# The first stage of a prime-factor Fourier filter on sixteen 32x32 tiles

## The chip, the cores and the metric

The kernel runs on one core of a Trainium2 chip. The metric is the device time of one launch in microseconds, the median of three runs. Everything is float32; a float32 matmul of the program appears in the trace as two matmul instructions.

## The reference

```python
batch, seq, dim = (8, 3008, 256)          # x; n_freq = 1505
X = np.fft.rfft(x, axis=1)
Y = X * (filt_r + 1j * filt_i)[None, :, :]
y = np.fft.irfft(Y, n=seq, axis=1)        # 24064 tokens of 256
h = y @ w_in                              # 256 -> 2048
g = h * np.clip(h + 3.0, 0.0, 6.0) / 6.0  # hardswish
out = g @ w_out                           # 2048 -> 256
```

Each of the 8 batches is filtered along its 3008 rows, every one of the 256 columns with a filter of its own. The filtered rows are the tokens of a two-layer network.

## The kernel before

**The network sets the order.** The 24064 tokens are 47 blocks of 512. A block is done in eight steps, one for each 256 of the 2048 hidden values, so there are 376 steps, numbered through; "step 42" is block 5, slice 2. In a step TensorE makes the seven products of a Strassen-like scheme for the first layer of its slice (`up_1` to `up_5`, tiles `al` and `be`) and the seven for the second layer of the slice before (`down`, tiles `po`). The last up-product of a step reads `xn` and writes `al`; it is the mark from which step lengths are counted here. ScalarE and VectorE make the hardswish. `t_sums` on GpSimd makes the operand sums of a block (`xt`), which the next block reads. Products go through `strips`, whose matmul is line 832.

**The filter is fitted between the steps.** 3008 is 47 x 64. For batch b:
- *First stage*, `a6_unit` (batches 2 to 7) and `a_unit` (batch 1): for each of the 64 residues c, a transform over the 47 rows 64a + c to frequencies k = 0 to 23, as matmuls with K = 47 against table `wa`, in which the twiddle factors are folded. A chunk of six columns is loaded by `x_load` and done by 12 matmuls of a 64x64 tile, 256 columns each; the last chunk of a batch has two columns and 4 matmuls. `a6_sums` makes sums and differences of the two halves on VectorE, `z6_store` writes them to DRAM (`z_d`) on GpSimd's queue. Batches 2 to 7 have six chunks each, at steps `A_AT` after the start of the seventh block ahead of the batch's first block.
- *Second stage*: `t2_load` reads z back, `b_unit` makes the 64-point transforms, `f_unit` and `y_unit` multiply with the filter on VectorE, `bi8_unit` makes the inverse 64-point transforms as 16 matmuls of a 32x32 tile with 512 columns, `bi8_sums` the sums of its halves, `g8_store` writes g to DRAM. The filter's rows come through `table_load` into two buffers `ft`: in batch 1 in 16 small transfers a table (lines 280 and 281) straight from the filter, and `table_store` then writes them to `f_d`; later batches read `f_d` in one transfer.
- *Last stage*: `t4_load` reads g (lines 731 and 742), `n_five` and `n_unit` make the last inverse transforms, whose output goes to `xn`, the tokens' ring.

Batch 0 goes through a path of its own before the steps; batch 1's first stage is in steps 2 to 9, its second in steps 12 to 34.

**Order by hand.** A dictionary `plan` says which functions a step calls and in which of five places. Place 3 stands at the beginning of a step, ahead of its up-products (`bi8_unit` stands there), place 4 just behind it, place 0 in the middle, place 1 later (`a6_unit`), place 2 at the end: loads, stores, sums. Within a place the order is that in which `at` was called. Each engine, and each queue of transfers, works through its instructions in this order. Transfers issued by `nc.sync` are on SP's queue: all loads, and the stores of the output in `store` (lines 1016, 1019 and 1024, once a block). Those by `nc.gpsimd` are on GpSimd's queue.

`late(i)` moves one VectorE operation (`g_last`) of a step that follows heavy VectorE work (`HEAVY`) behind `up_3`. After a unit in place 3, `inverse` picks the order of the down-products.

Of the kernel before, what the change touches and what calls it, by code (L numbers as in the profile page):

```python
# [42 lines left out]
SIX = tuple(range(0, HC, 6))  # L43
# [41 lines left out]
def _make_tables():  # L85
# [53 lines left out]
    def terms(k, j, at):  # L139
        m = (2.0 if k else 1.0) / N  # L140
        t0, t1 = ([2 * np.pi * ((at(j, h, a) * k) % N) / N for h in range(2)])
        c0, s0, c1, s1 = m * np.cos(t0), m * np.sin(t0), m * np.cos(t1), m * np.sin(t1)
        z = np.zeros(NA)
        if j:
            return {(0, 0): (c0, c1), (0, 1): (s0, -s1), (1, 0): (-c0, c1), (1, 1): (-s0, -s1)}
        return {(0, 0): (c0, z), (0, 1): (z, c1), (1, 0): (z, -s1), (1, 1): (-s0, z)}
# [11 lines left out]
    groups = np.zeros((P, HC, NA))  # L158
    ones = np.zeros((P, 2, TOK))
# [3 lines left out]
    for k in range(KH):  # L163
        for j in range(HC):
            for (ri, hh), x in terms(k, j, rows).items():
                if j in FIRST:
                    first[hh * 64 + ri * 32 + k, FIRST.index(j)] = first_of(x, FIRST.index(j))
                if j < 2:
                    ones[ri * ATOM + hh * KH + k, j] = cs_of(x)
            if j in FIRST:  # L170
                for (ri, hh), x in terms(k, j, late_rows).items():
                    last[ri * ATOM + hh * KH + k, FIRST.index(j)] = cs_of(x)
            if j > 1:
                cs = [terms(k, j, rows)[0, hh][0] for hh in range(2)]
                for ri in range(2):
                    c, s = cs[ri], cs[1 - ri]
                    pair_ = (c, s) if j < QC else ((c + s) / 2, (c - s) / 2) if j == QC else (c, -s)
                    for hh in range(2):
                        groups[ri * HALF + hh * KH + k, j] = pair_[hh ^ ri]
        if k >= KH - TC:  # L180
            for q in range(64):
                fr = k + NA * q if q < 32 else NA * (q - 31) - k
                for n, j in enumerate(FIRST):
                    th = [2 * np.pi * ((fr * rows(j, h, a)) % N) / N for h in range(2)]
                    direct[at_of[q], k - KH + TC, n * TOK:(n + 1) * TOK] = 2 / N * first_of(np.cos(th), n)
                    direct[HALF + at_of[q], k - KH + TC, n * TOK:(n + 1) * TOK] = -2 / N * first_of(np.sin(th), n)
    wai = np.concatenate([t.reshape(P, -1) for t in (groups, ones, first, last)], axis=1)
    f = np.float32
    return tuple(t.astype(f) for t in (wa, w0, wai, wi, wi2, wf, start, direct))


@with_exitstack
def kernel(
# [11 lines left out]
    wa_np, w0_np, wai_np, wi_np, wi2_np, wf_np, start_np, direct_np = _make_tables()  # L205
    wa_d = nc.inline_tensor(wa_np, name="wa_t").ap()
    w0_d = nc.inline_tensor(w0_np, name="w0_t").ap()
    wai_d = nc.inline_tensor(wai_np, name="wai_t").ap()
    wi_d = nc.inline_tensor(wi_np, name="wi_t").ap()
# [9 lines left out]
    f_d = nc.dram_tensor("f_tmp", (NT, P, TC * D), FP32, kind="Internal").ap()  # L219

# [39 lines left out]
    b12 = const.tile([P, P], FP32, name="b12")  # L260
    half_c = const.tile([P, 1], FP32, name="half_c")
# [34 lines left out]
    def table_store(c):  # L296
        nc.gpsimd.dma_start(f_d[c], ft[(NT + c) % FB].rearrange("p k d -> p (k d)"))
# [109 lines left out]
    def x_at(b, c):  # L407
        if b == 1:
            return xs[:, (b * NB + c) % 3, :, :], c * XC, XC
        t = xs.rearrange("p i j d -> p (i j) d")  # L410
        return t[:, ds((b * len(SIX) + c) % 2 * 6, 6), :], SIX[c], min(6, HC - SIX[c])

    def x_load(b, c):
        t, c0, n_ = x_at(b, c)
        rows = x[b].rearrange("(a c) d -> a c d", c=NC)
        for h in range(2):
            for r, n in ((0, 32), (32, NA - 32)):
                nc.sync.dma_start(t[h * 64 + r:h * 64 + r + n, 0:n_, :], rows[r:r + n, ds(h * HC + c0, n_), :])

# [58 lines left out]
    def a_unit(b, c):  # L482
# [8 lines left out]
        for h in range(2 if b == 1 and c < NB - 2 else 1):  # L491
            copy(c == NB - 2, t[:, :, h, :], ps[h])
# [3 lines left out]
    def a_sums(b, c):  # L496
        t, ps = st["t1", b, c]
        if b == 1:
            if c >= NB - 2:
                nc.vector.tensor_copy(out=t[:, :, 1, :], in_=ps)  # L500
            return
        nc.vector.tensor_tensor(out=t[:, :, 1, :], in0=t[:, :, 0, :], in1=ps, op=ALU.subtract)
        nc.vector.tensor_tensor(out=t[:, :, 0, :], in0=t[:, :, 0, :], in1=ps, op=ALU.add)

    def a6_unit(b, c):
        xc, c0, n = x_at(b, c)
        n //= 2
        t = t3p.tile([P, 4, 2, D], FP32, name="t3")[:, 0:3] if n == 3 else t1p.tile([P, 2, 2, D], FP32, name="t1")
        banks = [psF.tile([P, 512], FP32, name="psf", tag="f") for h in range(2)]
        be = psU.tile([P, 512], FP32, name="be") if n == 3 else None  # L510
        for r in range(n):
            for g in range(2):
                for h in range(2):
                    j, ps, o = (2, be, h) if r == 2 - 2 * h and n == 3 else (r - h if n == 3 else 0,) + (banks[h], r - h if n == 3 else 0)
                    q = g * n + j
                    nc.tensor.matmul(ps[ts(g, 64), ts(o, D)], wa[ds(h * 64, NA), ds((c0 + q) * 2 * KH, 64)],  # L516
                                     xc[ds(h * 64, NA), q, :], start=True, stop=True)
            if n == 3 and r == 0:
                nc.vector.tensor_copy(out=t[:, 2, 1, 0:2], in_=be[:, D:D + 2])
        m = min(n, 2)  # L520
        two = [ps[:, 0:m * D].rearrange("p (j d) -> p j d", d=D) for ps in banks]
        nc.scalar.activation(out=t[:, 0:m, 0, :], in_=two[0], func=AXT.Copy)
        if n == 3:
                nc.scalar.activation(out=t[:, 2, 1, 2:D], in_=be[:, D + 2:], func=AXT.Copy)
        st["t1", b, c] = t, be, two[1], n

    def a6_sums(b, c):
        t, be, ps, n = st["t1", b, c]
        v, m = nc.vector, min(n, 2)
        if n == 3:  # L530
            v.tensor_tensor(out=t[:, 2, 0, :], in0=be[:, 0:D], in1=t[:, 2, 1, :], op=ALU.add)
            v.tensor_tensor(out=t[:, 2, 1, :], in0=be[:, 0:D], in1=t[:, 2, 1, :], op=ALU.subtract)
        v.tensor_tensor(out=t[:, 0:m, 1, :], in0=t[:, 0:m, 0, :], in1=ps, op=ALU.subtract)
        v.tensor_tensor(out=t[:, 0:m, 0, :], in0=t[:, 0:m, 0, :], in1=ps, op=ALU.add)

    def z6_store(b, c):
        t, _, _, n = st.pop(("t1", b, c))
        for g in range(2):
            for ri in range(2):
                p0 = g * 64 + ri * KH  # L540
                nc.gpsimd.dma_start(z_d[b, :, ri, ds(SIX[c] + n * g, n), :, :].rearrange("k j s d -> k (j s d)"),
                                    t[p0:p0 + KH, 0:n, :, :].rearrange("p j s d -> p (j s d)"))
# [24 lines left out]
    def b_unit(b, i):  # L567
        c, r = divmod(2 * i, TC)
        if b != 1:
# [8 lines left out]
            else:  # L578
                for ri in range(2):
                    for s_ in range(2):  # L580
                        for v in range(2):
                            for k in range(2):
                                nc.tensor.matmul(ps[k][ds(v * 64 + s_ * 32, 32), ts(ri, D)], wf[ts(k, 64), s_, ts(ri, 32)],  # L583
# [66 lines left out]
    def bi8_unit(b, r):  # L650
        ys = [st.pop(("y", b, 2 * r + h)) for h in range(2)]
        even = [psU.tile([P, 512], FP32, name=x) for x in ("al", "be")]
        odd = [psF.tile([P, 512], FP32, name="psf", tag="f") for v in range(2)]
        for h in range(2):
            for ri in range(2):
                for v in range(2):
                    for par, ps in enumerate((even[v], odd[v])):
                        q = ds(v * HALF + par * HC, HC)
                        nc.tensor.matmul(ps[ds(h * HALF + ri * HC, HC)].rearrange("p (k d) -> p k d", k=2), wi2[q, ri, :],  # L659
# [384 lines left out]
    def at(step, fn, *a):  # L1044
        plan.setdefault((step, 0 if fn in EARLY else 1 if fn in (w_scale, a6_unit) else 2), []).append((fn, a))

    with tc.manual_schedule():
# [110 lines left out]

        def wai_load():
# [61 lines left out]
        A_AT = (4, 6, 10, 12, 14, 15)  # L1221
# [10 lines left out]
        at(n_at[TAIL - 2] + 1, lambda: nc.sync.dma_start(edge, wai_d[:, ds(NW + ND, ND)]))  # L1232
        at(LAST * NP + 3, b12_back)
        prev = None
        for n in range(1, B):
            a_at, f_at, y_at, bi_at = places(n)
            for c, s in enumerate(a_at):
                at(s, a_unit if n == 1 else a6_unit, n, c)
                at(s, a_sums if n == 1 else a6_sums, n, c)
                at(s, *((z_store, n, c, nc.sync) if n == 1 else (z6_store, n, c)))  # L1240
                if c >= (3 if n == 1 else 2):
                    at(max(a_at[c - 3 + (n > 1)], s - 6), x_load, n, c)
                elif n > 1:
                    at(max(prev[-1 if n == 2 else c - 2], s - 6), x_load, n, c)
            for c in range(NT):
                s = f_at[2 * (c - TB) + (n == 1)] + 1 if c >= TB else a_at[-1] + (1, 3, 5)[c] if n > 1 else a_at[-1] + 1
                at(s, t2_load, n, c)
                s = f_at[2 * (c - FB) + 1] + 1 if c >= FB else a_at[-1] + (1, 2, 4)[(c + 1) * (n > 1)]
                at(s, table_load, n, c)
                if n == 1:  # L1250
                    at(f_at[2 * c], table_store, c)
# [14 lines left out]
            prev = a_at  # L1266
# [3 lines left out]
        HEAVY = (f_unit, y_unit, a_sums, n_five, a6_sums, bi8_sums)  # L1270
# [5 lines left out]
        for i in range(len(items) + 1):  # L1276
# [23 lines left out]
            inverse = bi8_unit in units  # L1300
# [90 lines left out]
```

## Time and profile before

| | |
|---|---|
| runs | 2588.89, 2586.48, 2588.42; median 2588.42 us |
| profiled execution | 2587.13 us, span 2585.3 us, TensorE's clock 0.999 of full |
| TensorE busy | 2568.9 us, 99% |
| VectorE, ScalarE, GpSimd busy | 1926.3 (75%), 1291.5 (50%), 463.3 us (18%) |
| transfers | 202.48 MB, 121574 packets |
| first stage of batches 2 to 7 (L516) | 768 matmul instructions of 47x64 |
| inverse 64-point (L659) | 672 matmul instructions of 32x32, batches 1 to 7 |

Busy times are for the whole span; the DMA line of the page has the mean share of 16 engines in 40 slices of 65 us each. In groups of instructions the columns are line, engine, operation, output<-input, shape, count, then busy us, mean ns of one, and the engine's idle time before. In timelines they are start and length in us, engine, line, operation, output<-input, count; issues that follow one another are merged with their gaps.

### The profile page before, as it was taken

How to read it: one execution, taken by the hardware profiler on the slowest of the kernel's cores; microseconds unless marked ns; L12 is line 12 of the kernel's file. 1: busy time of each engine (PE TensorE's matmuls, PEld its weight loads, DVE VectorE, ACT ScalarE, POOL GpSimd, SP SyncE). 2: the span in 40 equal slices, each digit the busy share in tenths (PEclk: the TensorE clock that was granted, in tenths of full speed). 3: DMA queues.
4: the chain of work that ended last, by engine and by line, in shares of the span. 5: the costliest groups of instructions: out<-in, count | busy, mean ns of one | idle time of the engine just before them, and what ended most of it. 6: DMA issues, size and time to landing. Idle time of an engine off the chain costs nothing.

```text
span 2585.3 us, 87840 instructions
## 1 busy us (share of the span) xinstructions
PE 2568.9 (99%) x38466; PEld 2046.5 (79%) x38466; DVE 1926.3 (75%) x3554; ACT 1291.5 (50%) x2668; POOL 463.3 (18%) x699
## 2 busy tenths in 40 slices
PE   8999999999999999999999999999999999999999
PEld 4488778878788887888878878788777887888887
DVE  6978777777767777687776887767777677766666
ACT  4554455545545445554455545554445554555554
POOL 3252021110311203112031120311112111111110
PEclk9999999999999999999999999999999999999999
DMA  8733332222332223222232222322222222110000
GB/s 237 220 107 98 85 103 89 67 64 69 86 89 66 75 59 90 84 67 74 60 91 82 72 77 59 85 83 72 84 55 82 82 75 65 41 45 25 20 22 26
DMA packets 121574, 202.48 MB, mean 78 GB/s; under 512 B 18290, under 2 KB 86352, under 8 KB 120806
## 3 DMA queue, kind: packets, MB, share of 16 engines
q1 hardware_dynamic: 105453, 148.27, 20.0%
q0 software_dynamic: 15456, 48.35, 6.6%
q8 instruction: 302, 4.95, 0.8%
q14 instruction: 82, 0.67, 0.1%
q10 hardware_dynamic: 281, 0.24, 0.0%
HBM read 121.38 MB, written 87.13 MB: 81 GB/s over the span
## 4 chain that ended last, share of the span: by engine, by line
PE 99%; DVE 1%; issue 0%; ACT 0%; POOL 0%; POOLq 0%; DVEq 0%
PE po L832 45%; PE al L832 26%; PE be L832 19%; PE psf L583 1%; PE psn L772 1%; PE psf L516 1%; PE al L659 1%; PE al L772 1%; PE be L516 1%; PE psf L591 0%; PE psf L489 0%; PE psf L644 0%; PE psn L832 0%; PE po L576 0%; PE al L1093 0%
## 5 line engine op out<-in xcount | busy, mean ns | idle before, releaser
L832 PEld LDWEIGHTS po<-w_all,g 128*64 128x64 f32 x20808 | 1244.5, 137 | 247.2 <-issue 24.4
L832 PE MATMUL po<-w_all,g 128*64 128x128 f32 (+1 forms) x20808 | 1419.8, 274 | 1.5 <-issue 1.5
L885 DVE SCALAR_TENSOR_TENSOR g<-r,h 128x512 f32<-128x512 f32 x736 | 526.1, 715 | 221.1 <-ACT r L880 217.2
L880 ACT ACTIVATE r<-h,half_c 128x512 f32<-128x512 f32 x736 | 530.9, 721 | 306.4 <-DVE h L861 294.3
L832 PE MATMUL al<-xt,w_all 128*64 128x256 f32 x4416 | 668.7, 380 | 0.1
L832 PE MATMUL be<-xt,w_all 128*64 128x256 f32 x2944 | 444.8, 379 | 0.0
L861 DVE TENSOR_TENSOR h<-be,s 128x512 f32<-128x512 f32 x368 | 253.9, 690 | 164.8 <-PE be L832 146.8
L832 PEld LDWEIGHTS be<-xt,w_all 128*64 128x64 f32 x2944 | 213.8, 137 | 104.2
L875 ACT ACTIVATE h<-al 128x256 f32<-128x256 f32 x368 | 141.0, 383 | 288.1 <-PE al L832 285.2
L832 PEld LDWEIGHTS al<-xt,w_all 128*64 128x64 f32 x4416 | 280.2, 137 | 3.2 <-POOL w_all L393 1.0
L866 DVE TENSOR_TENSOR h<-al,s 128x256 f32<-128x256 f32 x368 | 156.3, 425 | 151.8 <-PE al L832 147.8
L893 DVE TENSOR_TENSOR g<-g 128x512 f32<-128x512 f32 x367 | 255.6, 697 | 12.6
L832 PE MATMUL al<-xn,w_all 128*64 128x256 f32 (+1 forms) x1536 | 240.7, 392 | 1.0 <-DVE g L885 0.6
L827 POOL TENSOR_TENSOR xt<-xn 128x256 f32<-128x256 f32 x184 | 140.9, 785 | 558.1 <-ACT xn L752 558.1
L832 PE MATMUL be<-xn,w_all 128*64 128x256 f32 (+1 forms) x1536 | 238.3, 389 | 0.0
L847 ACT ACTIVATE s<-be 128x256 f32<-128x256 f32 x368 | 141.1, 383 | 176.6 <-PE be L832 176.6
L856 ACT ACTIVATE s<-al 128x256 f32<-128x256 f32 x368 | 141.2, 384 | 174.6 <-PE al L832 174.5
L846 ACT ACTIVATE s<-al 128x256 f32<-128x256 f32 x368 | 141.8, 385 | 110.9 <-PE al L832 110.9
L892 DVE TENSOR_TENSOR g<-g 128x256 f32<-128x256 f32 x367 | 162.5, 443 | 12.6
L832 PEld LDWEIGHTS be<-xn,w_all 128*64 128x64 f32 x1536 | 110.1, 137 | 63.5 <-issue 7.4
L898 DVE TENSOR_TENSOR g<-g 128x256 f32<-128x256 f32 x367 | 156.1, 425 | 4.1
L676 POOL DMA_DIRECT2D g_tmp<-t x84 | 44.9, 544 | 586.0 <-DVE t L670 583.3
(171 smaller groups left out, 1720.5 us busy)
## 6 DMA issues: line engine op xcount, KB each, us to landing
g_tmp<-t POOLq DMA_DIRECT2D x96, 256.0 KB, 4.4
t<-z_tmp SPq DMA_DIRECT2D x42, 512.0 KB
t<-g_tmp SPq DMA_DIRECT2D x168, 120.0 KB
ft<-f_tmp SPq DMA_DIRECT2D x36, 512.0 KB
z_tmp<-t POOLq DMA_DIRECT2D x120, 144.0 KB, 3.7
o_tmp<-o SPq DMA_DIRECT2D x46, 256.0 KB
xs<-in_x_dram SPq DMA_DIRECT2D x60, 192.0 KB
out_dram<-o SPq DMA_DIRECT2D x165, 47.0 KB
```

Of the source, the lines that this page charges most:

```text
L832: nc.tensor.matmul(ps[ds(o, STRIP)], w[:, ds(o, STRIP)], x, skip_group_check=True, **kw)
L846: nc.scalar.activation(out=s[:, 0, :], in_=al, func=AXT.Copy)
L847: nc.scalar.activation(out=s5, in_=be[:, 1, :], func=AXT.Copy)
L856: nc.scalar.activation(out=s[:, 1, :], in_=al, func=AXT.Copy)
L861: nc.vector.tensor_tensor(out=st["h"][0].rearrange("p (a n) -> p a n", a=2), in0=be, in1=s, op=ALU.add)
L866: nc.vector.tensor_tensor(out=st["h"][1][:, 256:512], in0=al, in1=s5, op=ALU.add)
L875: nc.scalar.activation(out=st["h"][1][:, 0:256], in_=al, func=AXT.Copy)
L880: nc.scalar.activation(out=r, in_=st["h"][i], func=AXT.Relu, bias=half_c, scale=1.0 / 6.0)
L885: nc.vector.scalar_tensor_tensor(out=st["g", k, p][:, o:o + 2, :].rearrange("p a n -> p (a n)"), in0=st["r", i], scalar=1.0, in1=st["h"][i ...
L892: v.tensor_tensor(out=g[:, G1, :], in0=g[:, G3, :], in1=g[:, G22, :], op=ALU.add)
L893: v.tensor_tensor(out=g[:, G3:G2 + 1:2, :], in0=g[:, G3:G1 + 1, :], in1=g[:, G11:G11 + 1, :].broadcast_to([P, 2, 256]), op=ALU.subtract)
L898: nc.vector.tensor_tensor(out=g[:, G4, :], in0=g[:, G12, :], in1=g[:, G2, :], op=ALU.subtract)
```

## The change

For batches 2 to 7 the two transforms of 47 and 64 points are arranged in prime-factor order: row index n goes to (t, u) with n = 64t + 47u modulo 3008, and no twiddle factors are left between the stages. Rows that mirror each other in t (t and -t) then meet the same cosine and the opposite sine. So the first stage needs 24 sums (against cosines) and 24 differences (against sines) in place of 47 rows.

- `half_load` brings in, for 8 values of u at a time on four groups of 24 partitions, the rows and the mirrored rows: 8 transfers a chunk, 4 chunks a batch. `half_sums` makes sums and differences on GpSimd, four operations of 128x512.
- `a8_unit` does a chunk in 16 matmuls of a 32x32 tile (K = 24) over 512 columns, in place 3; `a8_sums` and `z8_store` take the places of `a6_sums` and `z6_store`. `A_AT` has four steps instead of six.
- Rows that wrap around the end of x are made contiguous by copies in DRAM: nine `x_twice` of 376 rows and eight `x_back` of 192 rows a batch, on SP's queue, some 50 to 30 steps ahead of their batch (for batch 2 from step 6).
- The frequencies are permuted, so the filter's tables are, too: 280 `filter_move`s copy runs of filter rows from the inputs to `f_d`, eight in each step from step 10 on, on SP's queue; in `plan` they stand behind `t4_load` and ahead of the other loads of their step. Batch 2 corrects signs (`table_sign`, VectorE) and stores the tables; batch 1 no longer stores them.
- Tables for the last stage are reloaded between batch 1 and batch 2 (`groups_load`); `wf2` and `wi2p` stand in for `wf` and `wi2`.

The diff, cut to its core:

```diff
+    def filter_move(n):
+        k, ri, par, (i, m, at_, step) = FILTERS[n]
+        c, r, v = k // TC, k // 2 % 2, k % 2
+        h = D // 2
+        o = c * P * TC * D + (v * HALF + par * 32 + i) * TC * D + (2 * ri + r) * D
+        nc.sync.dma_start(bass.AP(tensor=f_d.tensor, offset=f_d.offset + o, ap=[[h, 2], [TC * D, m], [1, h]]),
+                          raw((filt_r, filt_i)[ri], at_, [[h, 2], [step * D, m], [1, h]]))
+    def table_sign(b, c):
+        for r in range(2):
+            t = st["ft", b, c][:, 1, r, :]
+            nc.vector.tensor_scalar(out=t, in0=t, scalar1=sgn[:, ds(2 * c + r, 1)], scalar2=1.0, op0=ALU.mult, op1=ALU.mult)
+    def x_twice(b, i):
+        rows = lambda t, o: t[ds(o, XCUT)].rearrange("(r m) d -> r (m d)", m=4)
+        nc.sync.dma_start(rows(x_d[b - 2], i * XCUT), rows(x[b], (XLOW + i * XCUT) % N))
+    def x_back(b, i):
+        u = 8 * i
...
+        nc.sync.dma_start(xb_d[b - 2, :, ds(u, 8), :].rearrange("t u d -> u t d"), src)
+    def half_load(b, m, d):
...
+        for r in range(4):
+            u = 8 * m + 4 * (r % 2) + HC * (r // 2)
+            to = t[ds(32 * r, KH), :, :]
+            if d:
+                nc.sync.dma_start(to, xb_d[b - 2, :, ds(u, 4), :])
+                continue
...
+    def half_sums(b, m):
+        t0, t1 = halves(b, m)
+        s_ = slots[2]
+        for i in range(2):
+            u = ts(i, 2)
+            nc.gpsimd.tensor_tensor(out=s_[:, u, :], in0=t0[:, u, :], in1=t1[:, u, :], op=ALU.add)
+        for i in range(2):
+            u = ts(i, 2)
+            nc.gpsimd.tensor_tensor(out=t0[:, u, :], in0=t0[:, u, :], in1=t1[:, u, :], op=ALU.subtract)
-    def a6_unit(b, c):
...
-                    nc.tensor.matmul(ps[ts(g, 64), ts(o, D)], wa[ds(h * 64, NA), ds((c0 + q) * 2 * KH, 64)],
-                                     xc[ds(h * 64, NA), q, :], start=True, stop=True)
...
+    def a8_unit(b, m):
+        xs_ = slots[2], next(halves(b, m))
+        first_ = [psU.tile([P, 512], FP32, name=n) for n in ("al", "be")]
+        ps = first_ + [psF.tile([P, 512], FP32, name="psf", tag="f") for h in range(2)]
+        for ri in range(2):
+            for v in range(2):
+                for r in range(4):
+                    nc.tensor.matmul(ps[r][ds(ri * HALF + v * 32, 32)].rearrange("p (e d) -> p e d", e=2),
+                                     wcs[ds(32 * r, KH), ri, :], xs_[ri][ds(32 * r, KH), ts(v, 2), :], start=True, stop=True)
+        t = t3p.tile([P, 4, 2, D], FP32, name="t3").rearrange("p (r e) s d -> p r e s d", r=2)
+        for r in range(2):
+            nc.scalar.activation(out=t[:, r, :, 1, :], in_=ps[r].rearrange("p (e d) -> p e d", e=2), func=AXT.Copy)
...
-        A_AT = (4, 6, 10, 12, 14, 15)
+        A_AT = (4, 7, 13, 21)
...
+        for i in range(len(FILTERS)):
+            at(10 + i // 8, filter_move, i)
...
+                load = a_at[0] - 5 if c == 0 else a_at[c - 1] - 1
+                at(a_at[c] - 2, half_sums, n, c)
+                for d in range(2):
+                    at(load, half_load, n, c, d)
+                plan.setdefault((s, 3), []).append((a8_unit, (n, c)))
+                plan.setdefault((s, 4), []).append((a8_sums, (n, c, 0)))
+                at(s, a8_sums, n, c, 1)
+                at(s, z8_store, n, c)
+            for i in range(XCUTS if n > 1 else 0):
+                at(a_at[0] - (51 if n > 2 else 30) + 3 * i // 2, x_twice, n, i)
+            for i in range(8 if n > 1 else 0):
+                at(a_at[0] - (37 if n > 2 else 16) + i, x_back, n, i)
```

## The prediction

> **What bounds the kernel now.** I read the page first, then TensorE's timeline step by step, then the SP queue's timeline where the change adds transfers, then GpSimd's groups. The page (total, busy time, chain of waits):
>
> ```profile
> span 2585.3 us, 87840 instructions
> ...
> PE 2568.9 (99%) x38466; PEld 2046.5 (79%) x38466; DVE 1926.3 (75%) x3554; ACT 1291.5 (50%) x2668; POOL 463.3 (18%) x699
> ...
> PE 99%; DVE 1%; issue 0%; ACT 0%; POOL 0%; POOLq 0%; DVEq 0%
> ```
>
> TensorE is the chain from end to end and idles 16 us in all. So an edit is worth what it takes out of TensorE's stream, less what it makes TensorE wait. The stream is read off by steps: each step has one last up-product `al<-xn`, and the distance between two of them is the price of the step between.
>
> ```profile
> 353.93 0.60 PE L832 MATMUL al<-xn,w_all 128*64 128x256 f32 x4
> ...
> 360.00 0.60 PE L832 MATMUL al<-xn,w_all 128*64 128x256 f32 x4
> ...
> 367.72 0.65 PE L832 MATMUL al<-xn,w_all 128*64 128x256 f32 x4
> ...
> 500.04 0.60 PE L832 MATMUL al<-xn,w_all 128*64 128x256 f32 x4
> ...
> 501.45 0.61 PE L659 MATMUL al<-y,wi 32*32 32x512 f32 x1
> ...
> 507.48 0.65 PE L832 MATMUL al<-xn,w_all 128*64 128x256 f32 x4
> ```
>
> A bare step takes 6.08 (353.93 to 360.00). Step 42 carries an `a6_unit` of six columns: 360.00 to 367.72, 7.72. Step 63 carries a `bi8_unit`: 500.04 to 507.48, 7.44. In the same view step 47, with the two-column `a6_unit`, takes 6.82 (396.87 to 403.69), and the step after any of them 6.13. A unit on top of an `n_five` costs the same (9.18 against 7.54).
>
> **The change part by part.**
>
> *First stage on TensorE.* Removed per batch: five units at 7.72 - 6.08 = 1.64, one at 0.74, and 0.05 in each of six steps behind: 9.24 us. Added: four `a8_unit`. The trace does not have them, but it has their twin: `bi8_unit` is also 16 matmuls of a 32x32 tile over 512 columns in four banks, with two ScalarE copies and four VectorE sums of 128x512. So 7.44 - 6.08 = 1.36, plus 0.05 behind: 4 x 1.41 = 5.64. Gain 3.60 a batch, six batches: **21.6 us**. It lies wholly on the path.
>
> *VectorE and ScalarE.* Per batch VectorE had five times (2 x 0.43 + 2 x 0.68 + 0.16) and 0.84, 12.7 us; it gets 16 x 0.69 = 11.0. ScalarE's copies stay near 5 us. Both stay beside TensorE's work. `table_sign` adds twelve VectorE passes of 128x256 in batch 2; the nearest row is a 128x512 TENSOR_SCALAR of 0.47, so 0 to 5 us; VectorE is free a quarter of the time: I take 1.
>
> *GpSimd.* `half_sums` adds four 128x512 operations a unit. From these rows
>
> ```profile
> L827 POOL TENSOR_TENSOR xt<-xn 128x256 f32<-128x256 f32 x184 | 140.9, 785 | 558.1 <-ACT xn L752 558.1
> L393 POOL TENSOR_TENSOR w_all<-w_all 128x128 f32<-128x128 f32 x64 | 34.7, 562 | 18.2 <-DVE w_all L385 15.8
> ```
>
> (shape, count, busy us, mean ns, idle before) the line is 0.22 per 128 columns, so 1.23 for 512 and 4.9 us a unit. The tightest place is a batch's second unit, three steps behind the first. GpSimd first issues the first unit's z stores; behind a `bi8_unit` such four issues end 4.8 us into the next step (565.97, the step from 561.2). The sums end at 9.7; the unit starts 6.13 + 6.08 + 1.4 = 13.6 us into that stretch (1.4 is 500.04 to 501.45 above). Cover: 3.9 us, and `t_sums` behind it still ends a step before its use. I cost it at nothing; without that cover each microsecond would cost six.
>
> *The SP queue, once, in batch 1's stage.* Here the change adds most: 280 `filter_move`s, eight a step from step 10, plus `x_twice`, `x_back` and `half_load`. They stand in program order ahead of the filter and g loads of their step. This is the queue of before (start, length, line, count):
>
> ```profile
> 148.52 0.38 SPq L557 DMA_DIRECT2D t<-z_tmp  x1
> 148.96 0.67 SPq L280 DMA_DIRECT2D ft<-in_filt_r_dram  x1
> ...
> 174.12 6.09 SPq L742 DMA_DIRECT2D t<-g_tmp  x10
> ...
> 205.02 4.86 SPq L1019 DMA_DIRECT2D out_dram<-o  x7
> ```
> ```profile
> 256.30 6.60 SPq L1019 DMA_DIRECT2D out_dram<-o  x8
> 262.94 6.29 SPq L418 DMA_DIRECT2D xs<-in_x_dram  x8
> ```
>
> It issues without a break from 148.5 to 213.9, already, because batch 1's `table_load` is 16 issues of 0.64 each. What has to be out in time is `half_load` of batch 2's second chunk (step 35, behind 26 x 8 = 208 moves). Its unit stands at step 39. Without a stall step 36 begins at 318.7, then 7.44 + 6.13 + 7.54 give 339.8, the unit 1.4 later, the half that reads the differences 0.45 later: 341.7. Less 4.9 for the sums and 2.2 for landing (from a filter load's issue to its semaphore's last update in the trace): issued by 334.6. The queue is free from 146.5, so it has 188.1 us. Against that, from the timeline: tables, z and g loads 148.5 to 204.4, 55.9; store of block 1 6.3; four g loads 3.1; fifth table 11.5; sixth 10.9; stores of blocks 2 and 3 7.4 and 5.1; eight g loads 3.2; new half loads 16 x 0.41 = 6.6; fifteen new copies and a table x 0.44 = 6.6; and after each of three stores a pause of 3.0 (eight x loads took 6.29 where 8 x 0.41 = 3.3 would do). Sum 125.6. Left: 62.5 us, 0.30 a move. The queue's two waits of before (to 225.9 and 239.8, for a table's buffer) are gone by then, since it comes later than that.
>
> So TensorE waits 208 x f - 62.5, with f the time of a move in the queue. No row has such a move (two by up to 17 half rows, DRAM to DRAM). The rows near it (ns min/median/max):
>
> ```profile
> L731 SPq DMA_DIRECT2D t<-g_tmp x80: 289/314/1077, 210.8 to 2410.6; - x80
> ...
> L742 SPq DMA_DIRECT2D t<-g_tmp x200: 289/371/1793, 74.0 to 2305.7; - x100
> ```
> ```profile
> L280 SPq DMA_DIRECT2D ft<-in_filt_r_dram x24: 577/592/1602, 149.0 to 244.0; - x24
> ```
>
> With 0.045 between issues: 0.33 for the fastest, 0.36 for one-dimensional loads, 0.42 (0.44 in the mean from start to start, the odd long one included) for two-dimensional ones, 0.64 for pieces of the filter. A gain is excluded: an issue takes time and replaces none. I take **0.44**, the two-dimensional loads' mean, as the move has two dimensions: 91.5 - 62.5 = **29.0 us** of waiting, most at step 36, the rest at 39. Bounds: 0.33 gives 6, 0.64 gives 71. Behind the late half load the queue holds the g loads of step 38, which are due later; GpSimd, waiting for the half load, holds `t_sums` of block 5, whose 5.5 us still fit beside step 39's 7.4. At step 36 GpSimd's g stores (to 317.1) would make the unit 1.4 late by themselves; that lies inside the wait.
>
> [...]
>
> *Later batches.* The SP queue gets some 25 more issues a batch, 10 us in about 300, of which more than half are idle: nothing. That is 5 MB more data per batch, for engines whose digits on the page's DMA line are mostly 2 and 3 tenths: nothing. The x loads of batches 2 to 7 go, and `groups_load` reloads tables between batch 1's chunks, one issue each: nothing.
>
> *Sum.* -21.6 + 29.0 + 1 = +8.4 on the profiled run's 2587.1 (span 2585.3 and 1.8 around it). The median of the runs is 1.3 above that run: 2588.4 + 8.4 = **2597**.
>
> **The rivals.** *A, faster: the moves are cheap.* If a move costs 0.33 to 0.36, the wait is 6 to 12: 2588.4 - 21.6 + 10 + 1 = 2578. It decides from f = 0.37 down. For it: the 24-row loads at 0.36, and 60 us of idle queue between 214 and 320. Against: ten two-dimensional loads took 6.09, 0.61 each, in this very stretch. With moves at next to nothing it would be 2588.4 - 21.6 + 1 = 2568; no row is that low, and 0.02 of A's chance is for it. [...]
> *B, slower still: moves cost as filter loads,* 0.64: 2588.4 - 21.6 + 71 + 1 = 2639. For it: the same source rows; against: those loads write every second partition, moves none.
> *C: the sums on GpSimd run late in every batch.* If an add takes 3 us (VectorE's L885 rises from 0.69 to 0.93 us where GpSimd adds run beside it, so they do share something), 12 us exceed the 8.8 by 3: 6 x 3 on top, 2615. Against: GpSimd's adds have a longest of 1.23 at 256.
> *D: the new unit is no cheaper than the old,* 1.64: gain 14.9, 2604. Against: the twin's 21 units all cost 1.36 or a little more.
>
> **How the numbers follow.** Forecast (f 0.40 to 0.50, its own range 2589 to 2610) 0.45; A 0.30, B 0.14, C 0.07, D 0.04. The range reaches over A's and C's times and B's beginning: 2571 to 2625. 0.2% is 5.2 us, about what a measurement can tell from no change. Faster than that: A but for its upper edge, 0.28. Within: that edge and the third of the forecast near f = 0.40, 0.17. Slower: the rest, 0.55.
>
> **What would show it.** Steps with an `a8_unit` 7.44 long, their neighbours 6.1. The SP queue without a gap from 146 to some 390, moves about 0.44 apart. TensorE idle before the units of steps 36 and 39, released by GpSimd's sums, and those by a load; no such idle time from batch 3 on. Wrong would be: idle time before units of later batches (C), moves 0.35 or 0.6 apart (A, B), or a wait at another place, such as VectorE for `ft` in steps 12 to 30.

## The result and the profile after

The changed kernel takes **2691.8 us** (four runs, 2689.1 to 2697.2) where the one before takes 2587.5: a ratio of 1.041, 95% interval 1.039 to 1.043. I had forecast 2597, at most 2625. The page of the changed kernel (total, busy times, TensorE and its clock in 40 slices, chain of waits):

```profile
span 2691.7 us, 88272 instructions
...
PE 2586.7 (96%) x38466; PEld 2033.6 (76%) x38466; DVE 2001.1 (74%) x3500; ACT 1288.4 (48%) x2650; POOL 587.4 (22%) x747
...
PE   8998759999999999999999999999999999999998
...
PEclk9999879999999999999999999999999999999999
...
PE 85%; SPq 6%; DVE 6%; DMA 2%; issue 1%; ACT 0%; POOL 0%; POOLq 0%; DVEq 0%
```

TensorE was 99% of the chain; now SP's queue and VectorE have 6% each. The fourth to sixth slices of TensorE (8, 7, 5 tenths) are batch 1's stage, where I expected a wait, but a far longer one. VectorE's 6% are spread over all later batches, where I expected nothing.

The steps, as before by their last up-product, show that the unit itself is not the trouble. Step 87, which carries an `a8_unit`, and step 88 (TensorE's timeline):

```profile
744.53 0.60 PE L914 MATMUL al<-xn,w_all 128*64 128x256 f32 x4
...
752.12 0.65 PE L914 MATMUL al<-xn,w_all 128*64 128x256 f32 x4
...
758.25 0.60 PE L914 MATMUL al<-xn,w_all 128*64 128x256 f32 x4
```

It takes 7.59, the step behind it 6.13; I had 7.44 and 6.13. Comparing all 375 step lengths of the two traces splits the difference of the two spans, 106.4 us. (The split between units and sums takes the kernel both_out from below, which has the units but neither moves nor sums to speak of.)

| part | forecast | measured |
|---|---|---|
| units, steps 40 to the end | -21.6 | -19.1 |
| waiting up to step 39 (SP's queue) | +29 | +78.5 |
| `half_sums` on GpSimd, steps 40 to the end | 0 | +45.0 |
| behind the last matmul | 0 | +3.4 |
| signs (forecast); start-up (measured) | +1 | -1.4 |
| sum | +8.4 | +106.4 |

In both_out only 17.4 of the 19.1 lie in the steps that had or have a unit; the rest are a few other steps that happen to be shorter (step 306 by 1.1, step 100 by 0.7). The signs have no row of their own; what they cost lies in the other rows. Nor is all of the 78.5 idle time: up to step 39 TensorE is busy for 297.7 of 363.3 us, before for 283.5 of 284.9, so it idles 64 us more, and another 14 us are products at half clock: the granted clock is 0.50 for 6.8 to 20.5 us at each of the five longest waits, from a point within the wait on.

**Where SP's queue made TensorE wait.** Step 23 is 9.1 us longer than before, 29 13.9, 31 9.2, 36 23.7, 38 18.3. Waits in that stretch (engine and line, what released it, total, times, longest):

```profile
PE al L604 <- POOL xs L515: 20.4, 1, 20.4
...
PE psn L854 <- DMA t<-g_tmp: 17.0, 2, 15.9
...
DVE s L682 <- DMA ft<-in_filt_i_dram: 16.8, 2, 8.5
DVE s L682 <- DMA xb_tmp<-x_tmp: 14.0, 1, 14.0
```

Line 682 is `f_unit`: VectorE waits for batch 1's own filter tables in steps 23, 29 and 31, because the moves stand ahead of them. (In step 29 the trace names another transfer on the same semaphore.) The waits in steps 36 and 38 are those of the first unit and of an `n_five`. The cause is the price of a move, in the queue's row for `filter_move`:

```profile
L358 SPq DMA_DIRECT2D f_tmp<-in_filt_r_dram x140: 533/568/1880, 145.6 to 473.6; - x140
L358 SPq DMA_DIRECT2D f_tmp<-in_filt_i_dram x140: 533/567/2071, 148.2 to 477.3; - x140
```

The first 208 moves took 0.687 us from start to start in the mean (median 0.612): 208 x 0.687 - 62.5 = 80, against 78.5 longer in all and 64 of idle time. A row of the same kind stood in the profile of before, and the prediction leaves it out: line 1024, which copies output rows from DRAM to DRAM on the same queue.

```profile
L1024 SPq DMA_DIRECT2D out_dram<-o_tmp x18: 578/814/1124, 209.9 to 2542.4; - x18
```

Its shortest issue, 0.578, is near the moves' median of 0.568; its median, 0.814, would have been too dear.

**Where the sums made TensorE wait.** Step 86 takes 12.60 where 9.18 - 1.64 = 7.54 was due. All engines' timeline there:

```profile
728.47 2.36 POOL L622 DMA_DIRECT2D z_tmp<-t  x4 [19.04 <-DVE t L615]
...
730.81 2.55 POOL L515 TENSOR_TENSOR xs<-wa,xs 128x512 f32<-128x512 f32 x2
...
731.62 4.46 DVE L980 TENSOR_TENSOR g<-g 128x256 f32<-128x256 f32 x1
...
733.29 2.49 POOL L518 TENSOR_TENSOR wa<-wa,xs 128x512 f32<-128x512 f32 x2
...
736.13 1.07 PE L914 MATMUL po<-w_all,g 128*64 128x128 f32 x8 [3.16 <-DVE g L980]
736.99 1.07 PE L914 MATMUL al<-xt,w_all 128*64 128x256 f32 x4
```

The sums are on time (GpSimd is done at 735.8, the unit starts at 745.9). It is `g_last` on VectorE, line 980, that suffers: usually 0.42 us, here 4.46, and it ends 0.3 us after GpSimd's fourth operation. TensorE waits 3.16 us for it and then runs four microseconds at about half speed (1.07 for an up-product of 0.60; granted clock 0.56 from 736.1 to 740.0, 1.00 in the step before). The clock record has 0.50 for 3.41 us from 736.2 on; the wait of 1.63 us at 164.6 was followed by no half clock. In all the step is 5.1 us longer than due. In the other four later batches TensorE waits 3.16 or 3.17 us at the same place, and the step is 4.8 to 6.6 longer; in the two with 6.6 the half clock lasts 6.83 us instead of 3.41. The sums of the other three units cost about 0.9 each: there VectorE's `hswish` (line 967, 0.69) takes 1.76, twice in a row.

Lines 967 and 980, which are held, have two SBUF inputs; operations with one input in PSUM (lines 943, 948) keep their 0.69 and 0.42 in all 22 cases of each beside these sums. Beside memsets, which read nothing, `g_last` takes 0.41 (the run memset below).

### The profile page after: what moved, and what is told of

Same layout as the page of the kernel before. It is cut to its first block, busy times and chain, and to the rows that moved or that the text cites. A ratio compares the mean times of both kernels' runs of the same rounds, so it can differ in the third digit from the quotient of the medians.

```text
span 2691.7 us, 88272 instructions
## 1 busy us (share of the span) xinstructions
PE 2586.7 (96%) x38466; PEld 2033.6 (76%) x38466; DVE 2001.1 (74%) x3500; ACT 1288.4 (48%) x2650; POOL 587.4 (22%) x747
## 4 chain that ended last, share of the span: by engine, by line
PE 85%; SPq 6%; DVE 6%; DMA 2%; issue 1%; ACT 0%; POOL 0%; POOLq 0%; DVEq 0%
PE po L914 39%; PE al L914 22%; PE be L914 17%; SPq L358 3%; DVE g L967 2%; PE psn L854 1%; PE psf L664 1%; DVE g L980 1%; DMA out_dram<-o 1%; DVE g L974 1%; SPq L323 1%; PE al L604 1%; PE al L854 1%; SPq L324 1%; PE al L741 1%
## 5 line engine op out<-in xcount | busy, mean ns | idle before, releaser
L914 PE MATMUL po<-w_all,g 128*64 128x128 f32 (+1 forms) x20808 | 1438.8, 276 | 45.3 <-DVE g L967 26.9
L967 DVE SCALAR_TENSOR_TENSOR g<-r,h 128x512 f32<-128x512 f32 x736 | 564.9, 770 | 215.0 <-ACT r L962 207.1
L974 DVE TENSOR_TENSOR g<-g 128x256 f32<-128x256 f32 x367 | 182.9, 498 | 12.6
L980 DVE TENSOR_TENSOR g<-g 128x256 f32<-128x256 f32 x367 | 177.1, 482 | 4.1
```

The costliest lines, as they stand in the source:

```text
L914: nc.tensor.matmul(ps[ds(o, STRIP)], w[:, ds(o, STRIP)], x, skip_group_check=True, **kw)
L967: nc.vector.scalar_tensor_tensor(out=st["g", k, p][:, o:o + 2, :].rearrange("p a n -> p (a n)"), in0=st["r", i], scalar=1.0, in1=st["h"][i ...
L974: v.tensor_tensor(out=g[:, G1, :], in0=g[:, G3, :], in1=g[:, G22, :], op=ALU.add)
L980: nc.vector.tensor_tensor(out=g[:, G4, :], in0=g[:, G12, :], in1=g[:, G2, :], op=ALU.subtract)
```

## The experiments

**no_moves.** Six plain copies in place of the moves.

```diff
-        for i in range(len(FILTERS)):
-            at(10 + i // 8, filter_move, i)
+        for c in range(NT):
+            at(10 + 6 * c, filter_copy, c)      # f_d[c] <- 128 x 4 KB of a filter
```

> Changes part of the computation: the 280 filter moves are replaced by six plain copies of 512 KB into f_tmp (steps 10, 16, ... 40), so f_tmp has the same size but filter rows in another order. Theory (issue time of the moves on the SP queue is the whole one-time loss of 77 us at steps 23 to 38): those steps go back to within 1 us of the lengths before the change, time 2692 - 77 = 2615. Rival (the loss is the new traffic through x_tmp and xb_tmp or the late half loads themselves): stalls at steps 36 and 38 stay, time above 2660.

Measured 2620.9 (ratio to before 1.014). Steps 23, 29 and 31 are back to 6.94, SP's queue is at 0% of the chain:

```profile
PE 92%; DVE 6%; issue 1%; DMA 1%; ACT 0%; SPq 0%; POOL 0%; POOLq 0%
```

Steps 36 and 38 stay 3.8 and 6.1 us longer than in both_out: the sums, which the longer waits had covered. So 71 us net.

**tiny_sums.** Sums over 8 of 256 columns.

```diff
-nc.gpsimd.tensor_tensor(out=s_[:, u, :], in0=t0[:, u, :], in1=t1[:, u, :], op=ALU.add)
+nc.gpsimd.tensor_tensor(out=s_[:, u, 0:8], in0=t0[:, u, 0:8], in1=t1[:, u, 0:8], op=ALU.add)
```

(the subtractions alike)

> Leaves out most of the sums: half_sums works on 8 of 256 columns, its four GpSimd instructions, their waits and places stay. Theory (VectorE's operations with both inputs in SBUF are held while GpSimd's long sums run, 8 us a batch): steps with half_sums fall to the length of their neighbours (step 86 from 12.6 to about 7.5), time 2692 - 48 = 2644. Rival (the 8 us a batch come from the new unit's matmuls, its loads or its stores): time stays at 2692 within 8.

Measured 2651.0 (1.025). Step 86 is 7.54. The gain is 41 instead of 48; in steps 40 to the end it is 44; the start-up of this profiled run took 4.6 us longer. VectorE's share of the chain falls from 6% to 1%, SP's stays:

```profile
PE 90%; SPq 6%; DMA 3%; DVE 1%; issue 1%; ACT 0%; POOL 0%; POOLq 0%; DVEq 0%
```

**both_out.** Both cuts.

> Both cuts at once: six plain copies in place of the moves, and sums over 8 of 256 columns. If the two causes are all there is beside the units, 2692 - 77 - 48 = 2567, which is the time before less the 21.6 predicted for the units. If the units gain less (rival: no cheaper than the old ones), 2574 or more; if there is a third cost, more than 2575.

Measured 2572.3 (0.9945, 0.993 to 0.996). That is 5 above the 2567 and below both of the marks set, so the time alone does not tell which rival it is; the trace shows some of each. 3.4 us are a third cost behind the last matmul, as in the changed kernel. The units gain less: their steps are 2.6 us shorter in batch 2 and 3.0 in each later batch, instead of 3.6. Some other steps happen to be shorter by 1.7 in all. Up to step 40 the steps add up to within 0.1 us of before.

**cand.** Moves later, sums on VectorE.

```diff
-            at(10 + i // 8, filter_move, i)
+            at(10 + i // 3 if i < 78 else 36 + (i - 78) // 7, filter_move, i)
...
-                at(a_at[c] - 2, half_sums, n, c)
+                at(a_at[c] - 2, half_sums, n, c, 0)      # two additions, nc.vector
+                at(a_at[c] - 1, half_sums, n, c, 1)      # two subtractions, nc.vector
```

> Computes the same as the changed kernel: filter moves three a step in steps 10 to 35 and seven a step from 36 (78 moves ahead of step 36 instead of 208), and the sums on VectorE, two additions two steps before the unit and two subtractions one step before. Theory: 78 x 0.61 = 48 us of queue fit into the 62.5 us that were free, no stall; VectorE takes 16 x 0.69 = 11 us a batch beside TensorE, of which 0 to 4 us a batch show: 2567 to 2590, most likely 2572, faster than before. Rival (VectorE, 74% busy, becomes late for the products in each step that gets sums): 8 steps a batch of 1.4 us late, 2567 + 67 = 2634.

Measured 2596.2 (1.004, 1.002 to 1.005): above the theory's range, far below the rival. Up to step 35 there is no stall, but seven moves a step fill the queue from step 36 on, and batch 2's first table comes late. VectorE waits for it in step 53 (the waits from 430 to 446 us, same columns as above):

```profile
DVE ft L364 <- DMA ft<-f_tmp: 4.4, 1, 4.4
```

Step 53 is 14.43 long instead of 7.59. In each batch three of the four units start 1.0 to 1.6 us late, since the subtractions of the step before are not over. So the additions, two steps ahead, cost nothing; one step ahead is too near, but for a batch's first unit.

**to_sbuf.** The same 280 reads, but into SBUF.

```diff
-nc.sync.dma_start(bass.AP(tensor=f_d.tensor, offset=f_d.offset + o, ap=[[h, 2], [TC * D, m], [1, h]]), ...)
+nc.sync.dma_start(slots[3][ds(n % 4 * 32, m), n // 4 % 4, :], ...)
```

> Changes part of the computation: the 280 moves stay on the SP queue in their places and read the same filter rows, but write them into a free SBUF tile instead of f_tmp (which gets six plain copies at step 46). Theory (an issue costs 0.57 us because both ends lie in DRAM; loads from DRAM into SBUF cost 0.30 to 0.37 in the trace): an issue falls to about 0.35, the wait to 208 x 0.40 - 62.5 = 20 us or less, time 2692 - 77 + 20 = 2635. Rival (the rows of the filter or their shape set it, as in the filter loads of 0.59): issues stay at 0.57, time 2692 within 10.

```profile
L359 SPq DMA_DIRECT2D wa<-in_filt_r_dram x140: 244/318/1723, 145.7 to 435.9; - x140
L359 SPq DMA_DIRECT2D wa<-in_filt_i_dram x140: 228/316/2244, 147.4 to 438.3; - x140
```

The issue falls from 0.57 to 0.32, so it was not the filter's rows that made it dear. The run changes two things, though: the destination, and the pattern, which is whole rows here and two half rows in a move. The changed kernel's `x_twice` separates them: it copies whole rows from DRAM to DRAM and takes 0.538.

```profile
L486 SPq DMA_DIRECT2D x_tmp<-in_x_dram x54: 494/538/1995, 122.3 to 1767.0; - x54
```

So an issue with both ends in DRAM was dear here in either pattern: 0.57 and 0.54, against 0.32 into SBUF. The time, 2675.6, is neither theory's. From start to start an issue still takes 0.513 in the mean, since some last up to 2.2 us; by the formula that is 208 x 0.513 - 62.5 = 44 of waiting. Up to step 39 the steps are 49.0 longer than before, 34 of it idle time. (The six copies of step 46 add 12 in step 45.) I had put the median where the mean of a crowded queue belongs.

**memset.** GpSimd writes, but reads nothing.

```diff
-nc.gpsimd.tensor_tensor(out=s_[:, u, :], in0=t0[:, u, :], in1=t1[:, u, :], op=ALU.add)
+nc.gpsimd.memset(s_[:, u, :], 1.0)
+nc.gpsimd.memset(s_[:, u, :], 0.5)
```

> Leaves out the sums: each of the four GpSimd additions or subtractions becomes two memsets of the same 128x512 piece, which write SBUF and read nothing; by the 128x2560 memset of 2.23 us eight of them keep GpSimd busy for some 4 us, nearly as long as the sums. Theory (what VectorE and GpSimd share is the reading side): VectorE's operations keep their usual times, steps with memsets are not longer, time as with the short sums, 2651 within 4. Rival (any GpSimd run beside VectorE holds it, writes too): 8 x 4/5 = 6 us a batch stay, 2685.

Measured 2647.9, as tiny_sums within 0.2%. From step 85 on GpSimd's memsets stand beside an undisturbed `g_last`:

```profile
728.42 0.52 POOL L515 MEMSET xs<- 128x512 f32 x1
728.88 0.52 POOL L514 MEMSET xs<- 128x512 f32 x1
```
```profile
728.60 0.41 DVE L977 TENSOR_TENSOR g<-g 128x256 f32<-128x256 f32 x1
728.93 0.69 DVE L964 SCALAR_TENSOR_TENSOR g<-r,h 128x512 f32<-128x512 f32 x1
```

So VectorE was held beside sums that read (`g_last` 4.46 in the changed kernel), and not beside writes alone (0.41 here).

**pieces.** Eight sums over 256 columns instead of four over 512.

> Computes the same as the changed kernel: the four GpSimd operations of half_sums over 512 columns become eight over 256, back to back. Theory one (VectorE gets no turn between GpSimd operations that follow each other without a gap): as the changed kernel or worse by the longer total, 2692 to 2705. Theory two (VectorE gets its turn after each GpSimd operation, so that shorter ones hold it for 0.8 us instead of 1.3): half of the 48 us comes back, 2665.

Measured 2676.1, between the two: 17 of the 45 us from step 40 on come back. At three units in four VectorE gets its turn after each GpSimd operation, `hswish` takes 1.1 to 1.2, and the 0.9 us are gone. At the second unit it gets none, and nothing comes back (728.0 to 733.4):

```profile
727.57 2.83 POOL L515 TENSOR_TENSOR xs<-wa,xs 128x256 f32<-128x256 f32 x4
730.35 2.75 POOL L518 TENSOR_TENSOR wa<-wa,xs 128x256 f32<-128x256 f32 x4
```
```profile
728.38 5.01 DVE L980 TENSOR_TENSOR g<-g 128x256 f32<-128x256 f32 x1
```

What is special there is that the first unit's `z8_store` issues stand right ahead of the sums on GpSimd.

**z_sp.** On no_moves: those four issues go to SP's queue.

```diff
-                nc.gpsimd.dma_start(z_d[...], ...)
+                (nc.gpsimd if m else nc.sync).dma_start(z_d[...], ...)
```

> Changes part of the computation as no_moves does (six plain copies in place of the moves); beside that the first unit of a batch stores its z through SP's queue instead of GpSimd's, so that nothing on GpSimd stands right ahead of the second unit's sums. Theory (VectorE is kept out for a whole run of GpSimd operations only where these were queued up behind GpSimd's own DMA issues): step 86 keeps about 0.9 of its 3 to 5 us of excess, time 2621 - 25 = 2596. Rival (the place of the sums in the step decides): step 86 as before, 2621.

Measured 2592.0: 29 us faster than no_moves. Step 86 is 7.54, without even the 0.9 that I had left it. The sums also begin earlier now (at 647.8, in step 84 and not at the end of 85, with two VectorE operations that read PSUM beside them), so this run alone does not tell order from place.

**pool_moves.** All moves on GpSimd's queue, sums on GpSimd.

```diff
-            at(10 + i // 8, filter_move, i)         # nc.sync
+            at(10 + i // 5, filter_move, i)         # nc.gpsimd
```

> Computes the same as the changed kernel; only the queue and the rate of the moves change: GpSimd's queue, five a step from step 10, the sums stay on GpSimd. Theory (the one-time loss is SP's issue time alone, not the moves' data): as without moves, 2621, the 71 us come back and the 48 us of the sums stay. Rival (GpSimd, with moves, sums and t_sums, is late in batch 2): 2635 or more, with waits of TensorE in steps 36 to 65.

Measured 2629.8 (1.016, 1.014 to 1.018), between theory and rival. Up to step 35 every step has the length of before, so the 71 us were SP's issue time and not the data, which are the same (five moves a step instead of eight). The 9 us that are missing to 2621 are another case of the hold: moves now stand right ahead of the sums of all of batch 2's units. Steps 43 and 44 lose 6.4 and steps 51 and 52 4.7, where the same two units cost 0.9 each in no_moves. Step 38 (VectorE, then GpSimd):

```profile
338.58 7.67 DVE L967 SCALAR_TENSOR_TENSOR g<-r,h 128x512 f32<-128x512 f32 x1 [1.12 <-ACT r L962]
```
```profile
335.69 3.00 POOL L358 DMA_DIRECT2D f_tmp<-in_filt_i_dram  x5
338.71 2.52 POOL L515 TENSOR_TENSOR xs<-xs,wa 128x512 f32<-128x512 f32 x2
341.18 2.49 POOL L518 TENSOR_TENSOR xs<-xs,wa 128x512 f32<-128x512 f32 x2
```

The `hswish` even began 0.13 us ahead of the first sum, and was held through all four and the first three operations of `t_sums` behind them. It ended 0.5 us after the first gap in GpSimd's operations began, at 345.70.

**cand2.** Moves on GpSimd's queue as in pool_moves; sums on VectorE, one step earlier than in cand.

```diff
-                at(a_at[c] - 2, half_sums, n, c)
+                at(a_at[c] - (2 if c == 1 else 3), half_sums, n, c, 0)   # additions, nc.vector
+                at(a_at[c] - 2, half_sums, n, c, 1)                      # subtractions, nc.vector
```

> Computes the same as the changed kernel: all filter moves on GpSimd's DMA queue, five a step from step 10 (the last in step 65), and the sums on VectorE one step earlier than in cand (additions three steps before the unit, subtractions two; both two steps before the second unit). Theory: SP's queue is as free as without moves, GpSimd has 5 x 0.6 = 3 us a step for the moves, the sums are over when the unit starts, so the 1.0 to 1.6 us per unit that cand lost are gone: 2572 as with both causes out, up to 2582 where VectorE shows: faster than before. Rival (GpSimd falls behind with issues of 0.6 us or more ahead of its sums for the products): TensorE waits for GpSimd's t_sums in steps 10 to 65, above 2600.

Measured **2566.1 (0.992, 0.9906 to 0.9935)**: it computes the same and beats both kernels. That is 6 us below the theory's 2572; against both_out 3.7 of it lie behind the last matmul and 1.9 in the start-up. Its page and steps 87 and 88:

```profile
span 2564.6 us, 88233 instructions
...
PE 2548.6 (99%) x38466; PEld 2021.0 (79%) x38466; DVE 1984.9 (77%) x3596; ACT 1288.3 (50%) x2650; POOL 616.1 (24%) x931
...
PE 98%; DVE 1%; DMA 0%; ACT 0%; issue 0%; POOL 0%; POOLq 0%; DVEq 0%
```
```profile
658.70 0.60 PE L911 MATMUL al<-xn,w_all 128*64 128x256 f32 x4
...
666.25 0.65 PE L911 MATMUL al<-xn,w_all 128*64 128x256 f32 x4
...
672.37 0.60 PE L911 MATMUL al<-xn,w_all 128*64 128x256 f32 x4
```

The unit's step is 7.55, and the steps of a later batch's units gain 3.2 (2.9 in one batch). VectorE takes 16 sums of 0.69 a batch, and from batch 3 on only one of the steps with sums or units is longer than in both_out, by 0.2; GpSimd's 280 issues of 0.60 show nowhere.

## Why the prediction was wrong

- **Units: cheaper than the old ones, as forecast, but dearer than their twin.** 1.36 + 0.05 = 1.41 a unit was forecast. With the step behind, a later batch's unit takes 1.53 to 1.56 in the changed kernel and in both_out; in cand2 the first unit of a batch mostly takes 1.41, the other three 1.51. The old units' 1.64 and 0.74 came off as read. That leaves 17.4 us (both_out) to 17.9 (cand2) of the 21.6 in these steps. Rival D put the new unit at 1.64 + 0.05 and the gain at 14.9, so the truth lies between the two; what makes the 0.1 us a unit was not traced.
- **SP's queue: right that TensorE would wait, wrong in f and in the place.** The mis-sized term is f: 0.44, the mean of two-dimensional loads into SBUF, where 0.687 was measured. "No row has such a move" was the mistake: line 1024 goes from DRAM to DRAM, with 0.58 to 1.12 us an issue. Even rival B's 0.64 was low. The prediction also had ten loads at 0.61 each in this very stretch, and used them against A alone. The step's second fault is the place: I priced only the half loads' due time, and noted waits on `ft` merely as a sign of error; the tables' due times come first, and steps 23, 29 and 31 have 32 of the 78.5 us. A move at next to nothing (0.02 of A's chance) no run shows: the shortest issue of one took 0.533 in the changed kernel. With the measured f the formula 208 f - 62.5 gives 80 and, in to_sbuf, 44. TensorE's added idle time was 64 and 34; the products at half clock behind the waits, 14 and 15 us, which the formula does not know, bring it to 78.5 and 49.0. That 80 stands so near 78.5 is in part luck.
- **`half_sums` "at nothing": wrong, 45 us.** The working asked only whether GpSimd is done in time, and it is. What it left out is who runs beside it: VectorE's operations with two SBUF inputs (`hswish` 1.76 instead of 0.69, `g_last` 4.46 instead of 0.42). Rival C had the hint (line 885 at 0.93 instead of 0.69) but drew the wrong end from it: not GpSimd's sums get late, VectorE does, and TensorE waits for VectorE. A short wait was dear besides, through the clock behind it (0.50 for 3.41 us): 3.16 us of waiting made step 86 5.1 us longer.
- **Later batches, SP: right**; with the moves gone and the sums short (both_out), no step behind batch 2's units that has no unit of its own is longer than before by more than 0.4 us.
- **The end: 3.4 us not foreseen.**

The causes are shown by taking each out alone, both together and both mended. Not settled are why the hold lasts for a whole chain behind a DMA issue, and what makes the end longer.

## What to carry to other kernels

Price a transfer by the row with the same kind of both ends (here an issue took 0.57 us from DRAM to DRAM, 0.32 from DRAM to SBUF) and with the mean of a full queue (0.687 here, where the median was 0.612), and check every consumer that stands behind it, not only the new one. Before work is put on an idle GpSimd, list VectorE's operations with two SBUF inputs beside it: VectorE itself, two or three steps ahead, was the cheaper place here (cand2: 2566.1 us, from batch 3 on no step with sums or units over 0.2 us longer than in both_out). The 280 small transfers could go to GpSimd's queue, 0.60 us an issue, but not right ahead of a chain of sums like these on GpSimd (pool_moves: 6.4 and 4.7 us at two units that cost 0.9 each in no_moves).

## What the runs showed of the hardware

**A chain of GpSimd sums right behind a GpSimd DMA issue kept VectorE out to its end.** I sorted all chains of three or more GpSimd operations beside which VectorE has a `hswish` or an operation on `g`, in before, the changed kernel, no_moves, pieces, pool_moves, z_sp and cand2. Behind something else than a DMA issue there are some 400, and no VectorE operation in them took over 1.8 us. Right behind a DMA issue there are 29, and in 27 one took 3.9 to 7.7 us; it ended 0.3 to 0.6 us after GpSimd's last operation of an unbroken run. All 27 are `half_sums`; the two without such a hold are `t_sums` behind moves. So in the 27 VectorE was held through several GpSimd instructions; the runs do not show why.

**The end.** GpSimd's last drain takes 3.8 us in before, 7.8 in the changed kernel and in all that issue the same transfers on GpSimd's queue, whatever their sums; 5.8 in z_sp, which issues 24 fewer there, and 2.7 in pool_moves and cand2, which issue 280 more. So it goes with the transfers on that queue, but not simply with their number; how was not tried.
